# Attention, MLP and top-1 experts on one core: first expert's rows gathered ahead of the last token tile

## The chip, the cores and the metric

The kernel runs on one core of a Trainium2 chip. A core has a matrix engine (TensorE, PE in the profile), two engines for elementwise work that read and write both the on-chip memory (SBUF) and the matrix accumulators (PSUM) (VectorE, DVE; ScalarE, ACT), a third one that works on SBUF and issues indexed transfers (GpSimd, POOL), and an engine that issues the other transfers (SyncE, SP). All run their own instruction queues in order and wait for each other on semaphores. The metric is the device time of one execution in microseconds (us). The kernel before took 568.39 us in the median of three runs (563.79 to 570.07).

## What is computed

Three layers in a chain, in float32:

```python
def reference(q, k, v, w1, b1, w2, w_in, w_out, w_gate, e1, e2, capacity):     # shortened
    x = log1p(abs(i - j)) / log1p(max(i, 1))                  # 576 x 576 positions
    bias = relu(x[..., None] @ w1 + b1) @ w2                  # 32 hidden units, 8 heads
    p = softmax(q @ k.T / 8 + bias)                           # 2 batches, 8 heads, 576 x 64
    x = rows(p @ v)                                           # 1152 tokens x 512
    h = x @ w_in                                              # 512 -> 2048
    x = (h * tanh(log1p(exp(min(h, 20))))) @ w_out            # 2048 -> 512
    logits = x @ w_gate                                       # 8 experts
    e, g = argmax(logits), softmax(logits)[argmax]
    for each expert: the first 288 of its tokens, in order of token:
        out[token] = g * (relu(x[token] @ e1[expert]) @ e2[expert])   # 512 -> 1024 -> 512
```

A token whose expert already has 288 tokens gets zero.

## The kernel before

Tokens go through in five tiles, `it` 0 to 4. Tiles 0 to 3 hold 128 rows of each of the two batches (numbered t = 0 to 7, t = 2 it + batch); the last tile, it = 4 (t = 8), holds the last 64 rows of both. For each tile there are: the bias (hidden layer of 32 units over the distances, `bias_tile`: a relu with a per-partition bias for each group of hidden units, L299 on DVE or L498 on ACT, then matmuls L509 into PSUM, an eviction `rbe`, a round trip through DRAM `bscr`), attention (scores L567 and L570, minimum L584 on DVE, exponential L585 on ACT, transposes L593, products L657), the MLP (products L766 and L799 or L803, with w_in and w_out held as a high and a low f16 half that are made at the start from the weights' loads), and `emit_y` (transposes, gate logits, the argmax as a one-hot row `o3`, the rank of each token within its expert, the table `tbl` of slots scattered to DRAM, and the rows `yscr` of all tokens written to DRAM).

Up to that point the operations are not issued in the order in which they are written. A planner records each operation with its engine, a cost in nanoseconds, the buffers that it reads and writes and other engines that could do it. A table of numbers, `ORDER`, then says in which order the operations are issued; each number is eight times the operation's index plus the chosen alternative. Buffers come from rings: `R2` (row-sized SBUF buffers, `ra*` and `rw*`), `RB` (eight PSUM banks `pb*`, `ps*`), `RBE` and `RX` (the bias evictions and the MLP's input). A buffer is taken again when its last reader is done.

The expert stage stands behind it, in the order as written. `first_slots` gives the token numbers of the first expert's 288 slots: for each tile a one-hot of slots times token number is added up in `acc0` and `acc1` (L1008; one for each batch), the last tile has its own, and nine small matmuls (L1031) with a selector bring the sum to 96 rows by three columns, `gid0` (L1037). Then:

1. `gather(0)`: three indexed transfers of 96 rows of `yscr` each, issued by POOL (L1210).
2. `experts_list`: 14 small DVE operations give the list `lst` of experts that have tokens, which SP and the other engines load into registers.
3. `xt(0, c)`: four transposes on PE for each gathered block (L1223), and a split into a high and a low part (ACT, DVE; L1053, L1054) into `xT0`.
4. `gemm1(0)` (L1233, 96 products of 288 columns, four runs of 24 in the trace), `gemm2` (L1256), the scatter of the results; the loads, gather and weight splits of the next expert run beside them.

The weights of the first expert, `W1`, are split into high (ACT, L1086) and low (DVE, L1087) 128x1024 pieces by planned operations (`first_loads`).

## Time and profile before

| | |
|---|---|
| median of 3 runs | 568.39 us (563.79 to 570.07) |
| the profiled execution | 565.96 us, its span 564.2 us |
| mean granted TensorE clock | 0.949 of full speed |
| TensorE busy | 498.4 us (88%) |
| VectorE, ScalarE, GpSimd busy | 399.6, 349.6, 130.5 us |
| last product of the MLP's second layer ends | 433.57 us |
| first product of gemm1(0) starts | 454.04 us |

The rows below come from one profiled execution, and all times in them are microseconds from the start of its span. "PEclk" is the TensorE clock that was granted in a stretch, as a share of full speed. A row of the timeline gives the start of a run of like instructions, the time from its start to its end, the engine, the line of the kernel, the operation, out<-in, and how many there were (x4); in brackets stands the idle time of the engine before it, and what ended that.

### The profile page before, as it was taken

The page shows a single profiled execution, that of the slowest core. Times are in us where ns is not written, and L with a number is a line of the kernel's source. Part 1 is how long each engine was busy: PE and PEld are TensorE (multiplying, and loading weights), DVE is VectorE, ACT ScalarE, POOL GpSimd, SP SyncE. Part 2 cuts the span into 40 slices and gives each one's busy share as a digit, 9 for nine tenths or more (in the row PEclk, how much of TensorE's full clock was granted, in tenths as well). Part 3 has the DMA queues.
Part 4 walks back from the last instruction along what each step waited for, and adds up shares of the span by engine and source line. Part 5 has one row for each costly group of instructions (what it writes and reads, how often), then busy time and mean ns, then how long its engine had stood idle before and what let it go on. Part 6 is the DMA issues. An engine that isn't in the chain of part 4 may idle for free.

```text
span 564.2 us, 11689 instructions
## 1 busy us (share of the span) xinstructions
PE 498.4 (88%) x4412; PEld 359.6 (64%) x4412; DVE 399.6 (71%) x975; ACT 349.6 (62%) x705; POOL 130.5 (23%) x151
## 2 busy tenths in 40 slices
PE   4545798999999999999979999999998199999975
PEld 2211365686687564465757774699557189999963
DVE  5989999999865678668645875479766653837362
ACT  6879998878565768886726872356543153636251
POOL 4332124113001313100000325025232401131311
PEclk9778599999999999999989999999999579999998
DMA  8996975700200145224360002050006263373711
GB/s 292 377 339 218 362 249 182 279 10 1 81 22 24 66 133 178 86 82 168 111 146 29 1 3 88 3 205 2 1 21 243 70 227 123 105 271 97 283 34 31
DMA packets 28471, 73.96 MB, mean 131 GB/s; under 512 B 5126, under 2 KB 5254, under 8 KB 26352
## 3 DMA queue, kind: packets, MB, share of 16 engines
q1 hardware_dynamic: 26704, 68.95, 36.0%
q0 software_dynamic: 1696, 4.11, 2.4%
q8 instruction: 39, 0.64, 0.5%
q14 instruction: 32, 0.26, 0.2%
HBM read 55.67 MB, written 17.61 MB: 130 GB/s over the span
## 4 chain that ended last, share of the span: by engine, by line
PE 62%; DMA 10%; DVE 7%; issue 5%; ACT 2%; POOL 2%; SPq 0%; POOLq 0%; DVEq 0%; ACTq 0%
PE pb L799 13%; PE pb L766 12%; DMA xg<-yscr,gid 5%; PE ps L567 5%; PE pb L657 4%; PE ps L766 4%; DMA ra<-bscr 3%; PE py L1256 3%; PE pb L593 3%; PE ph L1233 3%; PE pt L1233 2%; PE pb L509 2%; PE pb L803 2%; PE ps L593 2%; PE ps L570 2%
## 5 line engine op out<-in xcount | busy, mean ns | idle before, releaser
L766 PEld LDWEIGHTS <-WIt 128*128 128x128 f16 x960 | 85.2, 98 | 13.2 <-issue 3.0
L766 PE MATMUL pb<-PX,WIt 128*128 128x256 f16 (+1 forms) x720 | 78.5, 264 | 1.1 <-ACT ra L596 1.1
L799 PE MATMUL pb<-WOt,ra 128*128 128x512 f16 x288 | 67.3, 379 | 0.0
L585 ACT ACTIVATE ra<-ra,rm 128x576 f32<-128x576 f32 x58 | 44.8, 774 | 14.2 <-DVE rm L584 14.2
L567 PE MATMUL ps<-AT,rq 64*128 64x512 f32 (+1 forms) x160 | 43.3, 673 | 8.3 <-DVE rm L584 8.3
L509 PE MATMUL pb<-ra,w2s 128*32 128x512 f32 (+16 forms) x232 | 32.2, 531 | 17.0 <-ACT ra L498 10.7
L498 ACT ACTIVATE ra<-AT,stab 128x576 f32<-128x576 f32 (+17 forms) x72 | 44.8, 661 | 3.1 <-DVE AT L299 2.3
L799 PEld LDWEIGHTS <-ra 128*128 128x128 f16 x288 | 27.7, 98 | 29.7 <-issue 1.5
L584 DVE CUSTOM_DVE_ANT_0 ra<-ps,ra 128x576 f32<-128x576 f32 x51 | 37.1, 752 | 12.7 <-DMA ra<-bscr 5.0
L299 POOL TENSOR_SCALAR rw<-rw 128x1024 uint32<-128x1024 uint32 (+1 forms) x19 | 25.8, 1357 | 66.6 <-DMA rw<-wo 28.8
L1256 PE MATMUL py<-HH,W 128*128 128x288 f32 x288 | 40.5, 298 | 0.0
L1054 DVE TENSOR_TENSOR W<-AT,W 128x1024 fp32r<-128x1024 f32 x28 | 33.7, 1223 | 9.3 <-ACT W L1053 4.9
L1256 PEld LDWEIGHTS py<-HH,W 128*128 128x128 f32 x288 | 38.9, 188 | 0.0
L657 PE MATMUL pb<-ra,AT 128*64 128x128 f32 (+1 forms) x640 | 37.4, 266 | 0.0
L657 PEld LDWEIGHTS pb<-ra,AT 128*64 128x64 f32 x640 | 32.2, 137 | 4.2 <-issue 3.4
L302 DVE SCALAR_TENSOR_TENSOR rw<-rw 128x1024 int32<-128x1024 int32 (+1 forms) x26 | 31.9, 1241 | 1.5 <-POOL rw L299 1.1
L593 PE MATMUL pb<-ident,ra 128*128 128x128 f32 x183 | 29.1, 290 | 1.4 <-ACT ra L585 1.0
L570 PEld LDWEIGHTS ps<-AT,rq 128*128 128x128 f32 (+1 forms) x80 | 10.8, 185 | 29.7 <-issue 29.0
L1053 ACT ACTIVATE W<-AT 128x1024 fp32r<-128x1024 f32 x28 | 29.0, 1055 | 0.0
L299 DVE TENSOR_SCALAR ra<-AT,stab 128x544 f32<-128x544 f32 (+16 forms) x46 | 22.6, 508 | 8.2 <-PE pb L799 5.7
L509 PEld LDWEIGHTS pb<-ra,w2s 128*32 128x32 f32 x232 | 7.3, 116 | 32.8 <-ACT ra L498 15.6
L596 ACT COPY ra<-pb 128x384 f32<-128x384 f32 x50 | 22.8, 478 | 6.9 <-PE pb L593 4.6
(404 smaller groups left out, 1084.7 us busy)
## 6 DMA issues: line engine op xcount, KB each, us to landing
AT<-m SPq DMA_DIRECT2D x32, 512.0 KB
bscr<-rbe SPq DMA_DIRECT2D x36, 295.5 KB
ra<-bscr SPq DMA_DIRECT2D x29, 288.0 KB
rw<-wo SPq DMA_DIRECT2D x8, 1024.0 KB
rw<-wi SPq DMA_DIRECT2D x4, 1024.0 KB
WOt<-wi SPq DMA_DIRECT2D x4, 1024.0 KB
AT<-k SPq DMA_DIRECT2D x4, 576.0 KB
out<-ra SPq DMA_DIRECT2D x9, 256.0 KB
```

The costliest lines, as they stand in the source:

```text
L299: eng.tensor_scalar(out=out, in0=in0, scalar1=s1, scalar2=s2, op0=op0, op1=op1)
L498: on_act = lambda h_=h_, g=g: act.activation(h_.t[:, 0:dn], T[:, 0:dn], AF.Relu, bias=stab[:, g:g + 1])
L509: pe.matmul(ps.t[32 * c:32 * c + 32, 0:d1 - d0], w2s, hs[c].t[:, d0:d1], start=True, stop=True)
L567: pe.matmul(s_.t[r, 1024 * i:1024 * i + 512], q_.t[hs, c], kraw[hs, k0 + 576 * bb:k0 + 576 * bb + 512], start=True, stop=True)
L584: op("DVE", c_dve(S), lambda i=i, own=own, m_=m_, b_=b_: dve.tensor_tensor_reduce(out=own(), in0=blk(s_.t[:, 960 * i:960 * i + S]), in1=bl ...
L585: op("ACT", c_act(S, 2), lambda i=i, m_=m_, col=col: act.activation(t_.t[:, S * i:S * i + S], t_.t[:, S * i:S * i + S], AF.Exp, bias=m_.t[ ...
L593: pe.transpose(pa.t[:, P * j:P * j + P], t_.t[:, 384 * n + P * j:384 * n + P * j + P], ident)
L657: pe.matmul(ov[64 * i:64 * i + 64, ct % 2, w * bb:w * bb + w], v_, t_.t[:, at + c0:at + c0 + w], start=n == 0, stop=n == 4)
L766: pe.matmul(ps.t[:, n * f_:n * f_ + n], WI[:, wv, ct, P * ft:P * ft + P], xt.t[:, xv, ct, 0:n], start=i == 0, stop=i == 11)
L799: pe.matmul(y_.t, gv()[:, g2, c:c + P], WO[:, wv, ft], **kw)
L1054: dve.tensor_tensor(out=dst[:, 1], in0=src, in1=dst[:, 0].bitcast(F32), op=ALU.subtract)
L1256: pe.matmul(ps[:, 0:SL], W2[:, wv, ft, P * dt:P * dt + P], HH[:, hv, ft], start=ft == 0 and i == 0, stop=ft == 7 and i == 2)
```

## The change

1. **Rows gathered ahead.** A new function `first_rows`, called with tile 3, counts the first expert's tokens of tiles t = 0 to 7 alone, and makes `gid0` from `acc0` and `acc1` without tile 8 (token numbers are held plus one, so that a slot that is empty so far gives row 0 of `yscr`). The three gathers are issued from there, into buffers of the ring `R2`. So that they don't read what is not written, the rows of tile 8 in `yscr` are set to zero early by two transfers of 64 rows.
2. **The last tile by a product.** `first_slots` no longer gathers. The gathered rows are multiplied by a diagonal matrix `dg` (96 by 288, one where a slot is filled by tiles 0 to 7), which transposes them and clears the empty slots at once (three products of 96 columns for each quarter of the 512 features, L1080), and to the same PSUM bank the product of tile 8's rows with their one-hot of slots is added (L1084, 288 columns, float32). The split goes straight from that bank to `xT0` (L1086, L1087). All of this is planned work now. `gather(0)`, `xt(0, c)` and their transposes fall away.
3. **Order behind it.** `gemm1(0)` stands ahead of the register loads that the branch on the number of experts needs; the loads of the list on SP stand ahead of it as before.
4. **Relus on GpSimd.** The relu of the bias tiles gets POOL as a third engine, and the high part of `W1` gets DVE as an alternative to ACT.
5. **Plan.** `PX` and `RBE` move to a pool of their own, which is closed ahead of `W1` and gives place to `xT0`; the planner's cost of a bias reload is 460000 instead of 294912; and the whole table `ORDER` is another one, made with waits for PSUM banks that several operations share.

```diff
-    416, 144, 152, 160, 176, 136, 168, 120, 200, 184, 112, 192, 64, 208, 128, 0, 16, 8, 304, 408, 72, 216, 232, 224,
+    136, 144, 168, 160, 152, 176, 184, 304, 120, 64, 312, 432, 240, 8, 0, 16, 72, 248, 112, 128, 208, 216, 224, 232,
...
-            op("DVE", c_dve(dn, 0.52, 1), on_dve, r=["T", "stab"], w=[h_], p=["Tfree"], lk=1, alt=[("ACT", c_act(dn, 1), on_act)])
+            on_pool = lambda h_=h_, g=g: ts(pool, h_.t[:, 0:dn], T[:, 0:dn], stab[:, g:g + 1], ALU.add, 0.0, ALU.max)
+            op("DVE", c_dve(dn, 0.52, 1), on_dve, r=["T", "stab"], w=[h_], p=["Tfree"], lk=1, alt=[("ACT", c_act(dn, 1), on_act), ("POOL", c_pool(dn, 0.83, 1), on_pool)])
...
+    def first_rows():
+        pn, pi_ = pl.buf(RB), pl.buf(RB)
+        def f():
+            for b in range(2):
+                for t in range(b, 8, 2):
+                    pe.matmul(pn.t[:, E * b:E * b + E], one, o3[:, t, 1], start=t == b, stop=t == b + 6)
...
+        def f():
+            for c in range(NCH):
+                for j in range(2):
+                    pe.matmul(pv(c), acc[j][:, CS * c:CS * c + CS], sel3[:, j], start=j == 0, stop=j == 1)
...
+            dve.tensor_tensor(out=smsk[:, 1], in0=pw[:, :, 1], in1=smsk[:, 0], op=ALU.mult)
+            dve.tensor_tensor(out=smsk[:, 1], in0=pw[:, :, 0], in1=smsk[:, 1], op=ALU.add)
+            ts(dve, gid0, smsk[:, 1], -1.0, ALU.add, 0.0, ALU.max)
+        for c in range(NCH):
+            x_ = pl.buf(R2)
+            op("POOL", 1100, lambda c=c, x_=x_: pool.indirect_dma_start(out=x_.t[:CS, 0:DM], out_offset=None, in_=yscr, in_offset=bass.IndirectOffsetOnAxis(ap=gid0[:, c:c + 1], axis=0)), r=["gid0", "yscr"], w=[x_], lk=0, late=2500.0)
+            xg0.append(x_)
...
     def first_slots(m_):
...
+        for ct in range(4):
+            ps = pl.buf(RB)
+            cc = slice(P * ct, P * ct + P)
+            def f(ps=ps, cc=cc):
+                for c in range(NCH):
+                    pe.matmul(ps.t[:, CS * c:CS * c + CS], xg0[c].t[:CS, cc], dg.t[:CS, CS * c:CS * c + CS], start=c == 0, stop=False)
+            op("PE", 170 * NCH, f, r=xg0 + [dg], w=[ps])
+            def f(ps=ps, cc=cc):
+                pe.matmul(ps.t[:, 0:SL], y_.t[:, cc], m_.t[:, 0:SL], start=False, stop=True)
+            op("PE", 490, f, r=[y_, m_], w=[ps])
+            op("ACT", c_act(SL, 0, 50), lambda ps=ps, ct=ct: act.activation(W["x"][:, 0, ct], ps.t[:, 0:SL], AF.Copy), r=[ps, "W1"], w=[("xh", ct)], alt=[("DVE", c_dve(SL), lambda ps=ps, ct=ct: dve.tensor_copy(W["x"][:, 0, ct], ps.t[:, 0:SL]))])
+            op("DVE", c_dve(SL), lambda ps=ps, ct=ct: dve.tensor_tensor(out=W["x"][:, 1, ct], in0=ps.t[:, 0:SL], in1=W["x"][:, 0, ct].bitcast(F32), op=ALU.subtract), r=[ps, ("xh", ct)], w=[("xl", ct)])
...
     table(0)
-    gather(0)
     experts_list()
...
-    for c in range(NCH):
-        xt(0, c, (PT + PO)[c % 4])
-    tokens(0)
     for k in range(1, E):
         ev[k] = nc.values_load(lst[0:1, k:k + 1], engines=[mybir.EngineType.SP], min_val=0, max_val=E - 1)
+    gemm1(0)
+    tokens(0)
     nv = nc.values_load(lst[0:1, E:E + 1], min_val=1, max_val=E)
```

Three places in the order show where the instructions stand. The first is POOL's queue at the start, behind its constants. Before, it holds only the first bit operations on the weights as they arrive (`rw`, `WOt`: w_in and w_out; a wait on DMAHW is one for a load):

```order
L299 TENSOR_SCALAR rw0_107<-rw0_107 128x1024 [waits DMAHW5_49]
L299 TENSOR_SCALAR rw0_107<-rw0_107 128x1024
L299 TENSOR_SCALAR rw1_108<-rw1_108 128x1024 [waits DMAHW6_49]
L299 TENSOR_SCALAR rw1_108<-rw1_108 128x1024
L299 TENSOR_SCALAR WOt_105<-WOt_105 128x1024 [waits DMAHW0_49] x2
```

In the changed kernel the same queue begins with relus of the bias (`ra<-AT,stab`), and another one stands behind two loads' worth of weights:

```order
L301 TENSOR_SCALAR ra3_112<-AT_103,stab_88 128x560
L301 TENSOR_SCALAR ra1_110<-AT_103,stab_88 128x448 [waits DVE_49]
L301 TENSOR_SCALAR ra9_118<-AT_103,stab_88 128x576
L301 TENSOR_SCALAR ra0_109<-AT_103,stab_88 128x352 [waits DVE_49,PE_49]
L301 TENSOR_SCALAR WOt_105<-WOt_105 128x1024 [waits DMAHW2_49]
L301 TENSOR_SCALAR WOt_105<-WOt_105 128x1024
L301 TENSOR_SCALAR WOt_105<-WOt_105 128x1024 [waits DMAHW5_49]
L301 TENSOR_SCALAR WOt_105<-WOt_105 128x1024
L301 TENSOR_SCALAR ra0_109<-AT_103,stab_88 128x432 [waits PE_49]
```

In all, 46 relus of the bias moved to POOL (24 fewer on DVE, 22 fewer on ACT). Ahead of the first attention minimum (L584, now L587), DVE has 9 of them instead of 19; ahead of the first exponential (L585, now L588), ACT has 32 instead of 41.

The second place is DVE's queue at the end of the last tile. Before, `gid0` came out behind one low part of `W1` and the last additions:

```order
L1087 TENSOR_TENSOR W1_4305<-AT_103,W1_4305 128x1024 [waits DMAHW4_49,Activation_49]
L299 TENSOR_SCALAR rm6_130<-rm6_130,e0s_177 128x1
L299 TENSOR_SCALAR rw1_108<-sl16_172,rm6_130,ids_175 128x288 [waits DVE_49]
L1008 TENSOR_TENSOR acc1_174<-acc1_174,rw1_108 128x288 [waits DVE_49]
...
L1036 TENSOR_TENSOR smsk_181<-pb1_140,smsk_181 96x3 [waits DVE_49,PE_49]
L1037 TENSOR_TENSOR gid0_182<-pb1_140,smsk_181 96x3 [waits DVE_49]
```

Now `gid0` comes first, and between it and tile 8's one-hot of slots (`rw2<-sl16,rm11`) stand the high and low parts of `W1`, five pieces in all with the one behind it, and tile 8's rank:

```order
L301 TENSOR_SCALAR gid0_185<-smsk_184 96x3 [waits DVE_49]
...
L1071 TENSOR_TENSOR rw2_108<-ident_82,smsk_184 96x288 [waits DVE_49]
...
L1137 CAST W1_4575<-AT_103 128x1024 [waits DMAHW1_49]
L1138 TENSOR_TENSOR W1_4575<-AT_103,W1_4575 128x1024 [waits DVE_49]
...
L1138 TENSOR_TENSOR W1_4575<-AT_103,W1_4575 128x1024 [waits DMAHW0_49,Activation_49]
L1138 TENSOR_TENSOR W1_4575<-AT_103,W1_4575 128x1024
L301 TENSOR_SCALAR rm11_130<-rm11_130,e0s_180 128x1 [waits DVE_49]
L301 TENSOR_SCALAR rw2_108<-sl16_175,rm11_130 128x288 [waits DVE_49]
L1138 TENSOR_TENSOR W1_4575<-AT_103,W1_4575 128x1024 [waits DMAHW5_49]
L1087 TENSOR_TENSOR xT0_4571<-pb0_142,xT0_4571 128x288 [waits Activation_49]
```

The third place is PE's queue ahead of the first expert's `gemm1`. Before, the transposes of the gathered blocks `xg1` and `xg2` (here the later two) and then gemm1 (`ph0<-xT0,W1`):

```order
L1223 MATMUL pt1_4820<-ident_82,xg1_4822 128x96 [waits DMASW2_49]
L1223 MATMUL pt1_4820<-ident_82,xg1_4822 128x96 x3
L1223 MATMUL po0_4817<-ident_82,xg2_4823 128x96 [waits DMASW3_49]
L1223 MATMUL po0_4817<-ident_82,xg2_4823 128x96 x3
...
L1233 MATMUL ph0_4813<-xT0_4824,W1_4305 128x288 [waits Activation_49]
L1233 MATMUL ph0_4813<-xT0_4824,W1_4305 128x288 [waits DVE_49]
```

Now, for each quarter (bank pb4, pb3, pb0, pb2), products of the three gathered blocks (`rw0`, `ra4`, `rw1`; DMASW is a wait for a gather) with `dg`, and the product of tile 8's rows:

```order
L1080 MATMUL pb4_146<-rw2_108,rw0_106 128x96 [waits DMASW0_49,DVE_49]
L1080 MATMUL pb4_146<-rw2_108,ra4_113 128x96 [waits DMASW1_49]
L1080 MATMUL pb4_146<-rw2_108,rw1_107 128x96 [waits DMASW2_49]
...
L1080 MATMUL pb0_142<-rw2_108,rw1_107 128x96
L1084 MATMUL pb0_142<-rw2_108 128x288 [waits DVE_49,Activation_49]
L1084 MATMUL pb3_145<-rw2_108 128x288
L1084 MATMUL pb4_146<-rw2_108 128x288
...
L1084 MATMUL pb2_144<-rw2_108 128x288
L1281 MATMUL ph0_4847<-xT0_4571,W1_4575 128x288 [waits DVE_49]
```

The 12 transposes became 16 products, and gemm1's first product now waits for the last low part of all four quarters.

## Rows read from the trace of the kernel before

**Rows 1.** Windows by stage: busy us (x instructions), clock, DMA share, GB/s.

```profile
core 0: us, PE busy (x) PEld busy (x) DVE busy (x) ACT busy (x) POOL busy (x), PEclk, DMA share, GB/s
0.00:70.00 70.00, 38.19 (x330) 17.55 (x330) 59.15 (x127) 58.82 (x105) 21.20 (x50) 0.78 0.88 317
70.00:434.00 364.00, 355.00 (x3323) 243.99 (x3315) 271.12 (x703) 239.18 (x514) 81.40 (x74) 1.00 0.29 94
434.00:454.00 20.00, 6.01 (x63) 4.51 (x63) 11.63 (x55) 3.47 (x8) 7.01 (x8) 0.60 0.21 57
```

**Rows 2.** Waits of PE up to 434 us: waited for, us, times, longest.

```profile
PE pb L509 <- ACT ra L498: 10.7, 3, 7.5
PE ps L567 <- DVE rm L584: 8.3, 5, 3.2
```

**Rows 3.** Timeline, from the end of the MLP to the first expert.

```profile
433.60 0.69 ACT L862 ACTIVATE rw<-pb,gl 128x512 f32<-128x512 f32 x1 [5.36 <-PE pb L803]
...
436.77 0.23 DVE L299 TENSOR_SCALAR rr<-pb,rr 128x8 f32<-128x8 f32 x1
...
439.91 1.22 DVE L1087 TENSOR_TENSOR W<-AT,W 128x1024 fp32r<-128x1024 f32 x1
...
445.80 8.17 SPq L1203 DMA_DIRECT2D tb<-tbl  x2
445.90 0.16 DVE L1037 TENSOR_TENSOR gid<-pb,smsk 96x3 uint32<-96x3 f32 x1
...
447.08 0.94 POOL L1210 DMA_INDIRECT xg<-yscr,gid  x1 [2.34 <-DVE fl L1166]
...
449.55 0.91 POOL L1210 DMA_INDIRECT xg<-yscr,gid  x1 [0.30 <-issue]
...
452.56 0.90 PE L1223 MATMUL po<-ident,xg 96*128 96x96 f32 x4 [0.31 <-DMA xg<-yscr,gid]
...
454.17 1.96 SPq L1047 DMA_DIRECT2D AT<-m  x4
...
457.68 0.41 ACT L1234 ACTIVATE HH<-ph 128x288 fp32r<-128x288 f32 x1 [3.69 <-PE ph L1233]
```

**Rows 4.** Timeline of PE, first two groups of gemm1(0).

```profile
454.04 5.63 PE L1233 MATMUL ph<-xT,W 128*128 128x288 f32 x24 [0.58 <-ACT xT L1053]
459.50 3.33 PE L1233 MATMUL pt<-xT,W 128*128 128x288 f32 x24
```

**Rows 5.** Windows around the same place (columns as in Rows 1).

```profile
438.00:454.00 16.00, 3.69 (x22) 2.62 (x21) 9.23 (x41) 2.22 (x5) 6.04 (x7) 0.50 0.26 70
454.00:458.00 4.00, 3.96 (x15) 3.66 (x16) 0.63 (x2) 0.32 (x2) 0.00 (x0) 0.50 0.76 212
458.00:460.00 2.00, 2.00 (x15) 2.00 (x15) 1.39 (x2) 1.33 (x3) 0.00 (x0) 0.88 0.98 389
```

**Rows 6.** Timeline of PE: float32 products of 128 columns; transposes of 96 columns.

```profile
62.53 0.79 PE L570 MATMUL ps<-AT,rq 128*128 128x128 f32 x2
...
84.96 0.49 PE L570 MATMUL ps<-AT,rq 128*128 128x128 f32 x2
...
506.87 0.88 PE L1223 MATMUL pt<-ident,xg 96*128 96x96 f32 x8
```

**Rows 7.** Instructions by line, 0 to 60 us: busy us, mean ns | idle before.

```profile
L299 DVE TENSOR_SCALAR ra<-AT,stab 128x560 f32<-128x560 f32 (+13 forms) x19 | 9.7, 544 | 2.0 <-PE pb L509 2.0
L299 DVE TENSOR_SCALAR WOt<-WOt 128x1024 int32<-128x1024 int32 (+1 forms) x3 | 2.1, 690 | 0.0
L498 ACT ACTIVATE ra<-AT,stab 128x464 f32<-128x464 f32 (+15 forms) x41 | 24.8, 667 | 3.1 <-DVE AT L299 2.3 <-PE pb L509 0.5 <-PE ps L509 0.3
```

**Rows 8.** Timeline of the first 40 us: POOL's weight pieces, a pair of DVE's relus.

```profile
12.41 5.05 POOL L299 TENSOR_SCALAR rw<-rw 128x1024 f32<-128x1024 f32 x4 [6.55 <-DMA rw<-wi]
...
13.90 2.47 DVE L299 TENSOR_SCALAR ra<-AT,stab 128x560 f32<-128x560 f32 x2 [1.95 <-PE pb L509]
...
32.91 3.37 POOL L299 TENSOR_SCALAR WOt<-WOt 128x1024 uint32<-128x1024 uint32 x2 [11.89 <-DMA WOt<-wi]
```

93 lines of the change are left out of this document (52 added, 41 removed), and 202 rows, old and new, of the table ORDER.

## The prediction

> **What bounds the kernel now.** I read the windows by stage first [rows 1]. From 70 to 434 us PE is busy for 355 of 364 us at full clock: nothing but fewer products could win more than 9 us there, and the change removes none. PE's idle time lies in two places: 31.8 us in the first 70, and 14 of the 20 us from 434 to 454. The waits of PE [rows 2] name the engines of the start: 10.7 us for ACT's relus, 8.3 us for DVE's minimum L584. Both engines are nearly full there, DVE 59.15 and ACT 58.82 of 70 us [rows 1], and so are the transfers, with a share of 0.88. POOL is busy for 21.20.
>
> The other place is a chain, read in the timeline [rows 3]. I count from T = 433.57, the end of the last product of the MLP. `gid0` is written from 445.90 to 446.06, which is T + 12.5; the first gather is issued at 447.08 and the third at 449.55. PE waits for the last one until 452.56, so it landed 3.0 us after the start of its issue, at T + 19.0. Transposes and split bring gemm1 to 454.04 [rows 4], T + 20.5. With PE nearly idle since T + 4.4, the clock that was granted is half [rows 5]: 0.50 from 438 to 458, 0.88 from 458 to 460, full behind it. So gemm1's first 24 products take 5.63 us and the next 3.33 [rows 4], and the first run ends at T + 26.1. That is the number to beat.
>
> **The change, tail.** What goes: tile 8's one-hot, its addition and the third selector product ahead of `gid0`, the wait of the gathers for it, and the 12 transposes. What comes, step by step:
>
> *gid0.* The argmax of tile 8 ends at 436.77 + 0.23 = T + 3.4, and in the new order stands ahead of `gid0` as before. Then come some 16 small DVE operations of 0.16 to 0.23 us [rows 3], two of them of 288 columns, of which I take 0.3 each: 3 us, and 0.5 for the six selector products and the way to PE and back. `gid0` is at about T + 6.9, 5.6 us earlier than before, while the order alone suggests more: the rows are ahead of tile 8's slots, but not ahead of its argmax.
>
> *Gathers.* Issue 0.4 us later at T + 7.3 and, at the spacing of (449.55 - 447.08) / 2 = 1.24, T + 8.5 and 9.8; the last lands 3.0 later, at T + 12.8, 6.2 us earlier.
>
> *One-hot of tile 8.* This is what is late next, as DVE's row order shows. Behind `gid0` stand four small operations and `dg` (1.2), three small ones (0.5), the copy of a high part (0.69, the price of a single-source piece of 1024 columns [rows 7]), a low part (1.22 [rows 3]), the rank's six (1.1), two more low parts (2.44) and the one-hot's two (0.55): 7.7 us, T + 14.6. If POOL's gathers hold DVE up, T + 15.5.
>
> *Products.* No row shows a float32 product of 96 or 288 columns into such a bank. From above: two of 128 columns take 0.49 at full clock and up to 0.79 at half [rows 6], so 0.25 and 0.40 for one, 0.18 and 0.30 for 96 columns, 0.55 and 0.89 for 288. All 12 and 4 take 4.4 us at full clock and 7.2 at half. From below: transposes of 96 columns, 0.88 / 8 = 0.11 [rows 6] at full clock and 0.90 / 4 = 0.23 at half [rows 3], 288 columns at three times that: 2.6 and 5.4. They are products and no transposes, so I take the upper row. Seven of the first nine follow the last landing: T + 12.8 + 2.1 = T + 14.9, the one-hot is there by then. Before, the clock rose about 4.4 us after steady work began (454.04 to about 458.5 [rows 4, 5]); the same here gives full clock from T + 17.2. By then 2.3 us of the last 6.2 (4 x 0.89 and 3 x 0.30, 4.5 in all) are done; the other 2.2 shrink to 1.4. Products end at T + 18.6. The copy to the high part and the low part take 0.41 each (ACT's 288 columns [rows 3]), 1.0 with the waits: gemm1 starts at T + 19.6, only 0.9 us earlier, but at full clock: its first 24 take 3.33 and end at T + 22.9 instead of 26.1. Gain 3.2.
>
> *Behind gemm1.* PE's two register loads now stand between gemm1 and gemm2. SP's two transfers and its loads of the list span 8.17 us [rows 3], of which I read at most 0.9 for one such load. PE's sequencer runs ahead of it, the list is written by T + 23: 0.3 us is left. SP's list comes later (T + 23 instead of T + 14.5), so the weights of the second expert, asked for at 454.17 = T + 20.6, start near T + 29. Their use is a whole gemm1 and gemm2 away: nothing, and up to 2 us where they meet the second gathers. Sum of the tail: -2.9. Its ends: the products at the lower price, rising early, give -6; at half clock throughout, with gemm1's first run still at 5.63, the products end at T + 12.8 + 2.1 + 4.5 = T + 19.4, gemm1's first run at T + 26.0: nothing.
>
> **The change, start.** DVE loses 10 relus ahead of the first minimum, 10 x 0.51 (9.7 us for 19 [rows 7]) = 5.1 us; ACT loses 9 x 0.60 (24.8 for 41) = 5.4 ahead of the first exponential, but three evictions and three weight pieces now stand ahead of it that came later before, 0.41 [rows 3] to 1.2 each, some 4. So of the two that bound the start DVE is relieved by 5.1 and ACT by 1 to 2 us there, and by the rest later. POOL has room (48.8 us of 70 idle), and a relu there costs about half of its 1.26 us for a 1024-column piece [rows 8]. At most 5 us is to be won, since DVE's evictions, the transfers (0.88 of the time) and POOL's own delay stand behind it; nothing, if the transfers set the pace. I take half: -2.5. The rest of the new plan (order, waits for banks, the dearer bias reloads) can win no more than 9 us between 70 and 434 and may lose as much; no row decides for a sign, and I set it at 0, with 4 either way.
>
> **What speaks against it.** Two relus on DVE took 2.47 us at 13.90 [rows 8] while POOL's four pieces ran from 12.41 to 17.46; the mean of a relu is 0.51 [rows 7], so each lost about 0.7. The Trainium skill, SBUF, section Who interferes with whom, says why: GpSimd shares a pair of ports with VectorE, held for a whole instruction, and a single-source VectorE operation in a two-port mode that meets it is blocked until it ends. The trace agrees with it in that row. With POOL running 21 relus more at the start, 9 relus and 4 weight pieces left on DVE could each lose 0.7, which is 9 us against the 5.1 won.
>
> **Sum.** -2.9 - 2.5 = -5.4 on the profiled 565.96 gives 560.6. The median of the runs shown is 568.39, 2.4 above that execution, so I say **563.0** for the median. What a measurement here can tell from no change is about 1%, 5.7 us.
>
> **The rivals.**
> *More than that (0.2).* The products run at the lower price and the clock is up early (-6), and the start wins all of 5: 568.4 - 11 = 557. For it: DVE and ACT end both waits of [rows 2]. Against it: the one-hot behind four pieces of W1.
> *No change (0.2).* The tail keeps its half clock (nothing won) and the start is paced by transfers: 567 to 570, say 568. For it: 0.88 in [rows 1]. This is also the case that the gathers are ahead on paper only: by the order, `gid0` waits for the same argmax.
> *Slower (0.2).* POOL's queue. A relu of the second bias tile stands behind four pieces of `WOt` from two loads; before, POOL sat 11.89 us waiting for `WOt`, until 32.91, and then worked 3.37 [rows 8]. If that load comes no earlier, the relu ends near 37, PE's products of that tile and all evictions behind it wait, and ACT and DVE stand idle in a stage that they bound. That costs up to 11.9; it decides from the 8 us that the start and the tail would win at best. At 8 to 14 lost in the start, beside the 2.9 of the tail: 573 to 579, or 570 if half of it is hidden; I put it at 574. The blocked ports above add to this case.
> *The forecast (0.4).* Own range 559 to 567.
>
> **How the numbers follow.** Leaving out about one in ten at each end, from half of the second case (below 555) to half of the slower one (above 573): 555 to 573. Faster by over 1% means under 562.7: the 0.2 of the first rival and a little over half of the forecast, 0.42. Slower by over 1% means over 574.1: somewhat over half of the last rival, 0.12. The rest, 0.46, is within 1%.
>
> **What would show it.** The tail: the third gather landing near T + 12.8, the first product of tile 8 near T + 15, gemm1 near T + 19.6 and its first 24 products in 3.3 us instead of 5.63. The start: the first minimum earlier than before, and DVE's and ACT's busy time of the first 70 us down by 3 to 5 us from 59.15 and 58.82, while POOL's rises by 12 or more. I am wrong on the tail if the one-hot or the low parts come later than T + 16, or if the clock stays at half into gemm1; on the start if PE waits for a relu of POOL, or DVE's relus take a microsecond each; and on the middle if PE's idle time from the first minimum to T differs by more than 4 us from the 9 of before.

## The result, and the profile after

| | before | changed |
|---|---|---|
| median of 17 runs | 567.57 us (560.06 to 570.66) | 571.55 us (567.41 to 575.52) |
| ratio to before, 95% interval | | 1.0113 (1.0075 to 1.0151) |
| span of the profiled execution | 564.2 us | 569.2 us |
| mean granted TensorE clock | 0.949 | 0.956 |
| TensorE busy | 498.4 us | 508.4 us |
| VectorE, ScalarE, GpSimd busy | 399.6, 349.6, 130.5 us | 410.0, 334.3, 223.9 us |
| last product of the MLP's second layer ends (T) | 433.57 us | 436.47 us |
| first product of gemm1(0) starts | 454.04 us | 459.57 us |

The changed kernel is slower by 1.1% (4.0 us by the medians, 6.4 by the ratio), where 563.0 and a gain of 5.4 were forecast. The time lies inside the range given; the change has the other sign. Its stages, in the columns of [rows 1]:

```profile
core 0: us, PE busy (x) PEld busy (x) DVE busy (x) ACT busy (x) POOL busy (x), PEclk, DMA share, GB/s
0.00:70.00 70.00, 39.28 (x321) 16.45 (x321) 54.22 (x106) 54.71 (x96) 57.32 (x60) 0.83 0.83 298
70.00:434.00 364.00, 355.83 (x3283) 243.05 (x3284) 280.30 (x701) 225.76 (x493) 137.47 (x107) 1.00 0.30 97
434.00:454.00 20.00, 9.75 (x114) 8.52 (x112) 13.86 (x56) 4.30 (x8) 7.96 (x7) 0.65 0.18 51
```

In the first 70 us DVE and ACT did lose the 4 to 5 us that the relus were to take off them (59.15 and 58.82 before). POOL did not gain 12 but 36. Now PE's waits up to 437 us (waited for, us, times, longest), to be read beside [rows 2]:

```profile
PE ps L512 <- POOL ra L301: 8.1, 1, 8.1
PE pb L473 <- DMA AT<-vm: 6.8, 2, 4.4
PE pb L463 <- ACT ra L500: 5.8, 1, 5.8
PE pb L512 <- POOL ra L301: 5.8, 4, 2.8
PE ps L570 <- DVE rm L587: 3.9, 2, 2.0
PE pb L512 <- POOL rw L301: 2.5, 2, 1.9
```

PE's waits for relus of POOL are 8.1 + 5.8 + 2.5 = 16.4 us, where before it waited for ACT's relus (10.7) and for DVE's minimum (8.3). Most of the new waits took the place of old ones: up to 90 us all waits of PE add up to 33.9 us here and to 32.9 before. So the waits name the engine, and what it costs has to come from the experiments. POOL's timeline of the start shows what it was doing:

```profile
8.88 19.55 POOL L301 TENSOR_SCALAR ra<-AT,stab 128x528 f32<-128x528 f32 x8 [3.14 <-DVE stab L301]
28.50 6.77 POOL L301 TENSOR_SCALAR WOt<-WOt 128x1024 uint32<-128x1024 uint32 x4
35.25 2.82 POOL L301 TENSOR_SCALAR ra<-AT,stab 128x432 f32<-128x432 f32 x1
43.14 12.55 POOL L301 TENSOR_SCALAR ra<-AT,stab 128x432 f32<-128x432 f32 x4
```

Eight relus take 19.55 us. The relu that stands behind four pieces of `WOt` ends at 38.07 (the forecast's "slower" rival said 37), but POOL is not waiting for the load ahead of it, as in [rows 8]: it is busy from 8.88 on. Four relus more end at 55.69, and that is where PE's longest wait ends, in its own timeline:

```profile
55.74 0.90 PE L512 MATMUL ps<-ra,w2s 128*32 128x416 f32 x1 [8.13 <-POOL ra L301]
```

By line, POOL up to 90 us (busy us, mean ns | idle before):

```profile
L301 POOL TENSOR_SCALAR ra<-AT,stab 128x352 f32<-128x352 f32 (+12 forms) x20 | 48.2, 2420 | 4.5 <-DVE stab L301 3.1 <-PE pb L512 0.9
```

One relu costs POOL 2.42 us. DVE's own relus there cost 0.54 before [rows 7]. The other 26 relus on POOL come later, in two groups:

```profile
L301 POOL TENSOR_SCALAR rw<-AT,stab 128x432 f32<-128x432 f32 (+10 forms) x14 | 26.0, 1865 | 28.0 <-PE pb L512 13.4 <-DVE rm L587 10.8 <-DVE WOt L304 3.4
L301 POOL TENSOR_SCALAR ra<-AT,stab 128x320 f32<-128x320 f32 (+8 forms) x12 | 20.2, 1685 | 14.3 <-PE ps L512 6.6 <-PE pb L660 6.6 <-PE pb L512 0.9
```

Their mean is 1.78 us, at about the same width (428 columns, 422 in the start). So of the 2.42 us some 0.6 belong to the crowded start and the rest to the relu itself.

The tail, in the timeline, to be read beside [rows 3] (T = 436.47 here):

```profile
442.85 0.17 DVE L301 TENSOR_SCALAR gid<-smsk 96x3 uint32<-96x3 f32 x1
...
443.94 1.30 POOL L1057 DMA_INDIRECT rw<-yscr,gid  x1 [6.53 <-issue]
...
444.44 0.68 DVE L1137 CAST W<-AT 128x1024 fp32r<-128x1024 f32 x1
445.16 1.23 DVE L1138 TENSOR_TENSOR W<-AT,W 128x1024 fp32r<-128x1024 f32 x1
445.54 1.65 POOL L1057 DMA_INDIRECT ra<-yscr,gid  x1 [0.30 <-issue]
...
447.22 2.36 DVE L1138 TENSOR_TENSOR W<-AT,W 128x1024 fp32r<-128x1024 f32 x2
...
447.49 1.73 POOL L1057 DMA_INDIRECT rw<-yscr,gid  x1 [0.30 <-issue]
...
449.74 0.37 DVE L301 TENSOR_SCALAR rw<-sl,rm 128x288 f32<-128x288 f16 x1
...
451.25 1.17 PE L1080 MATMUL pb<-rw,rw 96*128 96x96 f32 x4 [1.13 <-DMA rw<-yscr,gid]
...
454.34 3.08 PE L1084 MATMUL pb<-rw 128*128 128x288 f32 x6
...
457.90 0.68 PE L1084 MATMUL pb<-rw 128*128 128x288 f32 x2
...
459.06 0.46 DVE L1087 TENSOR_TENSOR xT<-pb,xT 128x288 fp32r<-128x288 f32 x1 [0.70 <-ACT xT L1086]
...
459.57 3.46 PE L1281 MATMUL ph<-xT,W 128*128 128x288 f32 x24 [0.99 <-DVE xT L1087]
```

`gid0` comes when it was expected, T + 6.4. The gathers' issues take 1.30 to 1.73 us instead of 0.91 to 0.94, the last block lands at T + 14.7 (PE goes on at 451.25), the products end at T + 22.1, and gemm1 starts at T + 23.1 instead of T + 20.5 before. Its first 24 products are short, 3.46 us, and end at T + 26.6; before, 5.63 us and T + 26.1. So the tail won nothing.

One warning for all that follows: single profiles of kernels with the same order up to T place T between 432 and 437 us. Times are therefore compared by medians and intervals, and inside a profile by marks that repeat well: the start of attention's first minimum (58.5 to 60.4 us in before and in the seven kernels that keep before's start), and the tail counted from T.

### The profile page after: what moved, and what is told of

Read it like the earlier page. It is cut to its first block, busy times and chain, and to the rows that moved or that the text cites. A ratio compares the mean times of both kernels' runs of the same rounds, so it can differ in the third digit from the quotient of the medians.

```text
span 569.2 us, 11778 instructions
## 1 busy us (share of the span) xinstructions
PE 508.4 (89%) x4433; PEld 364.2 (64%) x4433; DVE 410.0 (72%) x972; ACT 334.3 (59%) x677; POOL 223.9 (39%) x191
## 4 chain that ended last, share of the span: by engine, by line
PE 61%; POOL 13%; issue 12%; DMA 9%; DVE 3%; ACT 1%; SPq 0%; POOLq 0%; DVEq 0%; ACTq 0%
PE pb L802 15%; PE pb L769 12%; POOL ra L301 7%; PE pb L660 7%; DMA xg<-yscr,gid 5%; PE ps L570 5%; PE ps L769 5%; PE pb L596 4%; PE pb L512 3%; PE ps L596 2%; PE ps L573 2%; POOL rw L301 2%; PE pb L806 2%; POOL WOt L301 2%; POOL out L1290 1%
## 5 line engine op out<-in xcount | busy, mean ns | idle before, releaser
L301 POOL TENSOR_SCALAR ra<-AT,stab 128x352 f32<-128x352 f32 (+15 forms) x32 | 68.4, 2144 | 18.8 <-PE ps L512 6.6
L769 PE MATMUL pb<-PX,WIt 128*128 128x256 f16 (+1 forms) x672 | 71.8, 263 | 0.6 <-ACT ra L599 0.6
L588 ACT ACTIVATE ra<-ra,rm 128x576 f32<-128x576 f32 x62 | 47.8, 773 | 30.2 <-DVE rm L587 30.1
L802 PE MATMUL pb<-WOt,ra 128*128 128x512 f16 x276 | 64.5, 379 | 0.0
L587 DVE CUSTOM_DVE_ANT_0 ra<-ps,ra 128x576 f32<-128x576 f32 x53 | 38.4, 751 | 9.1 <-PE ps L573 5.9
L500 ACT ACTIVATE ra<-AT,stab 128x496 f32<-128x496 f32 (+17 forms) x57 | 35.4, 651 | 8.4 <-DVE stab L301 2.7
L301 POOL TENSOR_SCALAR rw<-AT,stab 128x432 f32<-128x432 f32 (+10 forms) x14 | 26.0, 1865 | 28.0 <-PE pb L512 13.4
L660 PEld LDWEIGHTS pb<-ra,AT 128*64 128x64 f32 x660 | 34.0, 137 | 2.7 <-issue 1.7
L1290 POOL DMA_INDIRECT out<-OC,tid x9 | 10.9, 1209 | 61.4 <-DVE OC L1296 33.7
L301 POOL TENSOR_SCALAR rw<-rw 128x1024 uint32<-128x1024 uint32 (+1 forms) x13 | 18.9, 1455 | 36.1 <-DMA rw<-wo 21.0
L769 PE MATMUL ps<-PX,WIt 128*128 128x256 f16 (+1 forms) x288 | 30.4, 259 | 0.0
L573 PEld LDWEIGHTS ps<-AT,rq 128*128 128x128 f32 (+1 forms) x80 | 10.7, 183 | 29.0 <-issue 29.0
```

What stands on the lines that cost most here:

```text
L301: eng.tensor_scalar(out=out, in0=in0, scalar1=s1, scalar2=s2, op0=op0, op1=op1)
L500: on_act = lambda h_=h_, g=g: act.activation(h_.t[:, 0:dn], T[:, 0:dn], AF.Relu, bias=stab[:, g:g + 1])
L587: op("DVE", c_dve(S), lambda i=i, own=own, m_=m_, b_=b_: dve.tensor_tensor_reduce(out=own(), in0=blk(s_.t[:, 960 * i:960 * i + S]), in1=bl ...
L588: op("ACT", c_act(S, 2), lambda i=i, m_=m_, col=col: act.activation(t_.t[:, S * i:S * i + S], t_.t[:, S * i:S * i + S], AF.Exp, bias=m_.t[ ...
L660: pe.matmul(ov[64 * i:64 * i + 64, ct % 2, w * bb:w * bb + w], v_, t_.t[:, at + c0:at + c0 + w], start=n == 0, stop=n == 4)
L769: pe.matmul(ps.t[:, n * f_:n * f_ + n], WI[:, wv, ct, P * ft:P * ft + P], xt.t[:, xv, ct, 0:n], start=i == 0, stop=i == 11)
```

## The experiments

### Which part costs: one part given back, one part alone

**The relus given back.** The changed kernel with each of POOL's 46 relus on the engine that had it before (18 to DVE, 28 to ACT); nothing else. In the table `ORDER` what is left of a number when it is divided by eight is the engine:

```diff
-    714, 898, 858, 842, 546,      # alternative 2: POOL
+    713, 897, 856, 841, 544,      # 0: DVE, 1: ACT
```

> The changed kernel, with the 46 relus that it runs on POOL given back to the engine that ran each before (18 to DVE, 28 to ACT), at the same places of the order; all else as in the changed kernel. Theory 1 (the relus on POOL are the loss: 20 of them took 48.2 us in the first 90 us, and PE waited 13.9 us for them): the last product of the MLP ends at 434 us or earlier instead of 436.5, and the time is 566 to 569. Rival (the new order itself costs it, wherever the relus run): the product ends at 436 to 438 and the time stays at 571 or above, since DVE and ACT get 46 relus back, some 27 us of work between them.

568.37 us, ratio 1.0020 (0.9990 to 1.0049). The loss is gone: the relus on POOL cost 1.0113 - 1.0020 = 0.9%, some 5 us. T lies at 435.4 in its profile, not at the 434 that was expected; one profile does not place T that closely. What is left, order, pool, waits for banks and new tail together, is worth nothing that can be measured.

**The tail alone.** The changed kernel's code with the order of before up to tile 8's argmax (so no relu on POOL), and the changed order behind it.

```diff
-    136, 144, 168, 160, 152, 176, 184, 304, 120, 64, 312, 432, 240, 8, 0, 16, 72, 248, 112, 128, 208, 216, 224, 232,
+    # the order of before, its numbers turned into those of the changed kernel, up to the argmax of tile 8
```

> The order of the kernel before up to the last tile's argmax (with the relus on DVE and ACT where they were), and behind it the tail of the changed kernel: gathers ahead, products, the same order of the last 59 operations. Theory 2 (the new tail wins nothing: products at half clock behind gathers that are issued slowly, and the second expert's weights come late): the last product of the MLP ends within 1 us of 433.6, gemm1 starts some 23 us behind it, and the time is 568 to 571, 0 to 3 above the kernel before. Rival (the forecast of the tail holds, and what was lost lies elsewhere): gemm1 starts 20 us behind it, the time is 564 to 565.

568.80 us, ratio 1.0007 (0.9979 to 1.0035). The tail's -2.9 is not there. T came at 437.2 in the profile, an execution of 571.86 us, and not within 1 us of 433.6. Gemm1 starts at T + 22.3, its first 24 products end at T + 25.7 (before T + 26.1).

**The relus alone.** The kernel before, and the same 46 relus on POOL, in before's places.

```diff
-alt=[("ACT", c_act(dn, 1), on_act)]
+alt=[("ACT", c_act(dn, 1), on_act), ("POOL", c_pool(dn, 0.83, 1), on_pool)]
```

> The kernel before, with its own order and tail, in which the same 46 relus run on POOL. Theory 1: PE waits for POOL's relus for 8 us or more, and the time is 571 to 577. Rival (POOL's relus are harmless, the order is the loss): within 1.5 us of the kernel before, 566 to 569.

592.23 us, ratio 1.0405 (1.0357 to 1.0452): 24 us slower, far above the 571 to 577 expected. PE's waits in that kernel (its relus are L281 and L480), and its first minimum:

```profile
PE pb L492 <- POOL ra L281: 13.1, 3, 6.3
PE ps L550 <- DVE rm L567: 8.5, 5, 3.1
```

```profile
69.21 0.75 DVE L567 CUSTOM_DVE_ANT_0 ra<-ps,ra 128x576 f32<-128x576 f32 x1
```

The first minimum stood at 59.04 before. In an order that was not made for them the same relus lose 24 us; in the changed kernel's own order they lose 5.

### What a relu on POOL costs, and why

**Only the first 20 given back**, those up to 90 us (6 to DVE, 14 to ACT); the later 26 stay on POOL.

```diff
-    714, 898, 858, 842, 546,      # the first 20 alone
+    713, 897, 856, 841, 544,
```

> The changed kernel, with only the first 20 of POOL's 46 relus (those that the trace shows up to 90 us) given back, 6 to DVE and 14 to ACT. If the loss of the relus lies in the start (PE waited 13.9 us for them there): 568 to 569, as with all 46 given back. If it lies in the later tiles (26 relus, PE waited 2.5 us): 571 or more.

569.48 us, ratio 1.0027 (0.9993 to 1.0062). That is close to giving all of them back: most of the loss lies in the start, and the later relus cost little. The first minimum says the same: 63.38 in the changed kernel, 60.75 and 60.53 with all and with 20 given back.

**Four forms of the relu.** The bias as a column or as a constant, one operation or two, by group of hidden units; the sums of the hidden layer are changed by this.

```diff
-ts(pool, h_.t[:, 0:dn], T[:, 0:dn], stab[:, g:g + 1], ALU.add, 0.0, ALU.max)
+g % 4 == 0: tensor_scalar(..., scalar1=0.25, scalar2=0.0, op0=add, op1=max)                 # L503
+g % 4 == 1: tensor_scalar(..., scalar1=stab[:, g:g + 1], scalar2=None, op0=max)             # L505
+g % 4 == 2: tensor_scalar(..., scalar1=0.25, scalar2=None, op0=max)                         # L507
+g % 4 == 3: as before                                                                       # L509
```

> The changed kernel with POOL's relus in four forms on lines of their own, to read what the price of 2.4 us hangs on (bias or the relu itself is left out in three of them): an added number and a maximum; a maximum with the per-partition column alone; a maximum with a number alone; and the full form, column and maximum. If the second operation is what is dear, the two single ones take about half, near 1.3 ns a column as the weight pieces do; if the per-partition column is, the two forms with a number do; if neither, but the meeting with DVE, all four stay near 5 ns a column.

A single execution, 565.48 us, so its time is not compared. By line and shape (busy us, mean ns | idle before), 576 columns of three forms and 432 of the fourth:

```profile
L503 POOL TENSOR_SCALAR ra<-AT 128x576 f32<-128x576 f32 x1 | 2.3, 2292 | 0.0
...
L509 POOL TENSOR_SCALAR rw<-AT,stab 128x576 f32<-128x576 f32 x1 | 2.2, 2215 | 0.0
...
L507 POOL TENSOR_SCALAR rw<-AT 128x576 f32<-128x576 f32 x1 | 1.8, 1822 | 11.3 <-DVE rm L594 11.3
...
L505 POOL TENSOR_SCALAR rw<-AT,stab 128x432 f32<-128x432 f32 x1 | 1.4, 1447 | 0.3 <-DVE ra L786 0.3
```

These rows are single instructions. Over all of a form behind 90 us, the full relu takes 4.0 ns a column, an added constant and a maximum 3.9, a maximum with a constant alone 3.1. So a bias column or a constant makes no difference, and the second operation costs 0.4 to 0.5 us at 576 columns. The form with the column and a maximum alone scatters too much to be placed (1447 ns here, 2698 for the same shape in the start).

What stays is most of it: 1822 / 576 = 3.2 ns a column for one maximum. POOL's pieces of the weights, from which the price was taken [rows 8], are called bit operations in the section on the change, but the kernel has arithmetic there: two multiplications by constants in float32 (`WOt` in rows marked f32, 1339 ns for 1024 columns in the changed kernel, 1.3 a column), or a multiplication and an addition on whole numbers (uint32, 1814 ns, 1.8 a column). So the same instruction, in float32 and with two operations as well, is three times as dear when it adds and takes a maximum. An addition alone in float32 was not run, so how the price divides between the two is known only from the second operation's 0.4 to 0.5 us.

**All 46 relus in the cheapest form**, a maximum with a constant, in the same places of the same queues; the hidden unit's bias is left out.

```diff
-ts(pool, h_.t[:, 0:dn], T[:, 0:dn], stab[:, g:g + 1], ALU.add, 0.0, ALU.max)
+pool.tensor_scalar(out=h_.t[:, 0:dn], in0=T[:, 0:dn], scalar1=0.25, scalar2=None, op0=ALU.max, op1=ALU.bypass)
```

> The changed kernel with GpSimd's 46 relus in the one form that was cheapest in relu_price, a maximum with one constant and nothing added (the bias of the hidden unit is left out there), in the same places of the same queues. If the price of a GpSimd relu is what costs the time, its 20 relus up to 90 us fall from 48.2 us to about 34 to 37 (1.7 to 1.85 each), the first minimum of attention comes near 60 us instead of 63.4, and the time falls from 571.5 to 567 to 569 (a ratio to before of 0.999 to 1.003), as when the relus are given back. Rival: the place of the relus in GpSimd's queue, behind the weights' loads, sets it whatever they cost; then the first minimum stays at 62.5 or later and the ratio at 1.009 to 1.011.

564.42 us, ratio 0.9940 (0.9906 to 0.9974). POOL up to 90 us, and the first minimum:

```profile
L502 POOL TENSOR_SCALAR ra<-AT 128x352 f32<-128x352 f32 (+12 forms) x20 | 32.4, 1640 | 2.7 <-DVE AT L301 1.6 <-DVE rm L587 0.5 <-PE pb L512 0.3
```

```profile
60.51 0.75 DVE L587 CUSTOM_DVE_ANT_0 ra<-ps,ra 128x576 f32<-128x576 f32 x1
```

With the same queue and the same places, a relu of 1.64 us instead of 2.42 makes 7 us of difference by the medians (1.7% by the ratios). PE's waits for relus of POOL up to 90 us fall from 13.9 us to 0.6, and POOL now waits for loads of `WOt` and `rw` (up to 7.6 us at once) and still is not late. So the price counts, and the place behind the loads does not. How much of the difference is the price's is less sure: the first relu need not wait for the column of biases and starts at 7.33 instead of 8.88 us, more than half of the 2.9 us by which the first minimum moves, and the hidden values are others.

The kernel is also 0.8% faster than with the relus given back (0.9940 against 1.0020), some 4.5 us, more than was expected. This is not the gain that the forecast looked for in the start: the first minimum comes at 60.5 here and at 60.7 there. In the two profiles the difference lies between that minimum and T (369.4 against 374.7 us), where PE's idle time explains 2.4 us of it. What earns it stays open.

### Where the tail's gain went

**The splits of W1 ahead of T.** The tail alone, and the high and low parts of `W1` at before's places, ahead of T, so that DVE does little while the gathers are issued.

```diff
-    ... 14376, 14616, 14584, 14552, 14512, ...      # 14456 to 14512: the pieces of W1, among tile 8's work
+    ... 13616, 14472, 13896, ...  13656, 14480, 12136, ...      # where before has them
```

> The kernel with the old order and the new tail (568.8), in which the splits of W1 stand on ACT and DVE where the kernel before has them, ahead of the end of the MLP, instead of behind gid0. Theory 3 (DVE's W1 pieces slow down POOL's issue of the gathers, 1.3 to 1.7 us each instead of 0.93, and so make the rows late): each gather is issued in 0.91 to 0.95, the last one lands within 12.8 us of the MLP's end, gemm1 starts 1 to 2 us nearer to it than the 22.3 of that kernel, and the time is 567 to 568. Rival (the issue is slow for another reason): the same issue times and the same 22.3.

567.67 us, ratio 1.0008 (0.9967 to 1.0048). The gathers:

```profile
440.14 0.94 POOL L1038 DMA_INDIRECT rw<-yscr,gid  x1 [2.21 <-DVE n L302]
441.39 0.93 POOL L1038 DMA_INDIRECT rw<-yscr,gid  x1 [0.31 <-issue]
442.62 0.91 POOL L1038 DMA_INDIRECT ra<-yscr,gid  x1 [0.30 <-issue]
```

All three issues take 0.91 to 0.94. In the tail alone they took 0.94, 1.39 and 0.94, the second of them beside DVE's cast and a low part, and the scatter of the table behind them 1.76 beside two low parts, 1.02 here; in the changed kernel, with the same tail, all three ran beside DVE's pieces and took 1.30, 1.65 and 1.73. ACT's pieces were done before the gathers in both. So it is DVE's pieces that stretch the issue. The Trainium skill, SBUF, section Who interferes with whom, says that an indexed transfer which stalls beside a VectorE operation is one for which GpSimd could not get the shared ports while it writes descriptors; these rows agree with it. The same section infers that a two-input VectorE operation does not do this; the issue of 1.73 us ran beside two of those, so here the measurement decides. But little came of it: the last block lands at T + 13.6, not within 12.8, where it was T + 14.0 in the tail alone and T + 14.7 in the changed kernel, and gemm1 starts at T + 21.6, 0.6 earlier than in the tail alone and not 1 to 2. That is too little to be measured: 14 of the 16 products still stand behind the landing and set the end.

**Another order of the products.** In the changed kernel each quarter waits for all three blocks. Here tile 8's four products stand first (they need no gathered row), then for each block the four products of the four quarters; the one-hot of tile 8 is ahead of `dg`. Nothing else differs from the kernel above.

```diff
-for ct in range(4):
-    for c in range(NCH): matmul(ps, xg0[c], dg)       # 3 products of 96 columns
-    matmul(ps, y_, m_)                                # tile 8, 288 columns
+for ct in range(4): matmul(pss[ct], y_, m_)           # tile 8 first
+for c in range(NCH):
+    for ct in range(4): matmul(pss[ct], xg0[c], dg)   # as each block lands
```

> The same as the run with W1 early, with the products in another order: tile 8's four first, as soon as its one-hot is there, while the gathers are still on their way, then for each gathered block its four products at once; the one-hot stands ahead of the diagonal matrix on DVE. Theory 4 (the tail is bound by the 16 products that run at half clock behind the last landing, 7 to 8 us): only four products are left behind the last landing, gemm1 starts 16.5 to 18 us behind the MLP's end instead of 20.5 (before) and 23 (changed), at full clock: 562 to 564.5. Rival (the time is in what stands behind the products, or the start takes it back): above 566.

564.73 us, ratio 0.9936 (0.9897 to 0.9974). PE's timeline (T = 434.46):

```profile
443.99 4.18 PE L1058 MATMUL pb<-rw 128*128 128x288 f32 x8 [2.61 <-DVE nb L1048]
447.97 2.50 PE L1062 MATMUL pb<-rw,rw 96*128 96x96 f32 x16
450.30 1.06 PE L1062 MATMUL pb<-rw,ra 96*128 96x96 f32 x8
452.77 4.89 PE L1262 MATMUL ph<-xT,W 128*128 128x288 f32 x24 [1.42 <-DVE A L282]
```

Gemm1 starts at T + 18.3. PE works while the gathers fly, and the work behind the last landing (T + 13.7) shrinks from 14 products to the 12 small ones. Four had been expected there and a start at T + 16.5 to 18; tile 8's products, at half clock, last until 447.97 = T + 13.5. Nor does gemm1 run at full clock: the clock had risen (0.89 from 451 to 453), PE then waited 1.42 us, and from 453 to 455 it is 0.50 again, so the first 24 products take 4.89 us. Still, this run is faster than both kernels.

**The expert list while the gathers fly.** The same, with `experts_list` planned ahead of the products instead of behind the split.

```diff
+    op("DVE", 2200, experts_list, r=["cnt", "m64", "k64"], w=["lst"])
-    experts_list()
```

> The same as the run with the products in another order, and the list of experts is worked out while the gathers are on their way instead of behind the last low part. Theory 5 (SP gets the list late in the changed kernel, so that the second expert's weights and rows are late by about 1.4 us): the second expert's gemm1 starts 27.3 to 27.8 us behind the first gemm1 plus gemm2's start, as before, PE waits for no weights there, and the time is 0.5 to 1.5 below that run. Rival (the second expert's stall has another cause): no difference.

563.27 us, ratio 0.9939 (0.9905 to 0.9973): the same as without it. The list, and SP's loads behind it, are not what bounds here.

**gid0 ahead of tile 8's logits.** The additions, `gid0` and the gathers do not need tile 8, so they are moved ahead of its gate logits; the gathered blocks' products stand ahead of tile 8's, and two low parts of `W1` behind the one-hot.

```diff
+    first_rows and the three gathers, ahead of the logits of tile 8 (operations 1545 to 1551)
```

> The order of tail_list, with what belongs to tiles 0 to 7 moved ahead of the last tile's logits: gid0 and the three gathers are issued before the argmax of tile 8, the products of the gathered blocks (block by block) stand ahead of those of tile 8's rows, and two low parts of W1 stand behind the one-hot of tile 8. All work is done. If the start of gemm1 is set by the gathers (issue behind tile 8's argmax, T + 7), they are now issued near T + 4, land near T + 9, the products end near T + 13 and gemm1 starts near T + 14.5 instead of T + 18.3 of tail_order: 560 to 562 us. Rival: tile 8's own chain (argmax, rank, one-hot, and the low parts of W1 now behind it) sets it; then gemm1 starts no earlier than T + 17.5 and the time stays at 563 to 566.

565.15 us, ratio 0.9942 (0.9907 to 0.9978): no faster, although gemm1 starts at T + 15.4 and gemm2 at T + 28.3 (before T + 35.5). PE shows where it went:

```profile
433.81 1.50 PE L787 MATMUL pb<-ra,WOt 128*128 128x128 f16 x24
435.15 0.34 PE L1011 MATMUL pb<-o,one 128*128 128x8 f16 x8
437.36 0.43 PE L1027 MATMUL pb<-sel,acc 128*96 128x2 f16 x6 [1.86 <-DVE acc L999]
437.65 1.56 PE L787 MATMUL pb<-ra,WOt 128*128 128x128 f16 x24
```

The selector products of `gid0` (L1027) stood in PE's queue ahead of the last 24 products of the MLP, and waited 1.86 us for the additions. The MLP's products stop at 435.31 and go on at 437.65, so T itself came 2.3 us later.

**Products that nobody reads, to hold the clock.** The kernel above with 22 products of 288 columns in PE's gaps between T and gemm1.

```diff
+    for i in range(8):
+        pe.matmul(fb.t[:, 0:SL], one, sl16, start=True, stop=True)     # three places: 8, 6 and 8
```

> The kernel ahead, with 22 more products of 288 columns whose result nobody reads, in three of PE's gaps between the end of the MLP and gemm1. If PE's idleness there is why the granted clock falls, and the fall is what makes the products and the first group of gemm1 long, the clock stays at or near full, the float32 products take less, and the first group of gemm1 takes 3.3 us instead of 4.9: 1.5 to 4 us less than ahead. Rival: the clock falls all the same, or the added products stand in the way of the real ones: not less than ahead, up to 2 us more.

564.67 us, ratio 0.9965 (0.9929 to 1.0002): no gain. The windows (clock: third value from the end) show why:

```profile
438.00:442.00 4.00, 3.04 (x34) 2.31 (x31) 1.10 (x8) 0.69 (x1) 2.07 (x3) 0.53 0.21 57
442.00:446.00 4.00, 3.77 (x25) 2.72 (x26) 1.94 (x11) 0.77 (x3) 2.28 (x3) 0.50 0.35 98
446.00:450.00 4.00, 4.00 (x33) 3.44 (x31) 3.05 (x19) 0.00 (x0) 0.45 (x1) 0.50 0.85 157
450.00:454.00 4.00, 4.00 (x19) 3.86 (x18) 3.86 (x16) 0.00 (x0) 0.98 (x1) 0.50 0.48 106
```

The clock had fallen by 440, before T and right behind the wait of 1.87 us for the additions; the first added product ran at 443.56, behind tile 8's logits. The first 14 of the 22 came at half clock too (8 in 2.13 us), and only the last 8, ahead of gemm1, at full (1.14 us). They filled PE and moved the real ones back (gemm1 at T + 17.1). Whether an earlier filler would hold it was not tried.

**The selector products behind the MLP.** The kernel with `gid0` ahead, and only those six products moved behind the last 24.

```diff
-    ..., 1547 (selector products), 1780 (the MLP's last 24 products), ...
+    ..., 1780, 1547, ...
```

> The kernel ahead, with the six selector products of gid0 moved behind the last 24 products of the MLP in PE's queue. In ahead they stood in front of these 24, and PE waited 1.86 us there for the additions into acc (VectorE's one-hots, GpSimd's sums), so that T itself came later by about that; gemm1 followed T by 15.4 us instead of 18.3, and the time was that of tail_order. If that wait is what gave the gain back, gid0 now comes about T + 1.2, the gathers are issued from T + 1.5, the products of the gathered blocks still start with dg near T + 6, gemm1 follows T by 15 to 16 us, and the time falls by the 1.9: a ratio to before near 0.990 to 0.991 (561 to 562 us by a before of 567). Rival: the three microseconds of ahead's tail are lost elsewhere (by the loads of the second expert, or by POOL and DVE in the last tile); then the ratio stays at 0.994.

562.91 us, ratio 0.9881 (0.9842 to 0.9920). The same place (T = 430.63):

```profile
429.13 1.50 PE L787 MATMUL pb<-ra,WOt 128*128 128x128 f16 x24
431.14 0.43 PE L1027 MATMUL pb<-sel,acc 128*96 128x2 f16 x6 [0.51 <-DVE acc L999]
...
436.66 3.73 PE L1061 MATMUL pb<-rw,rw 96*128 96x96 f32 x16 [1.22 <-DVE rw L1052]
440.18 1.91 PE L1061 MATMUL pb<-rw,ra 96*128 96x96 f32 x8
441.89 3.43 PE L1064 MATMUL pb<-rw 128*128 128x288 f32 x8
```

The MLP runs through, gemm1 still starts at T + 15.7, and the kernel is the fastest of all, 1.2% under before: the idea of the change, with no relu on POOL and with the products and `gid0` in other places. The profile is of one of its fastest executions (555.96 us), so T itself is not compared here.

The tails and the times agree when they are put side by side. From gemm2's start on, PE waits for only some 4 to 5 us in each, so what gemm2 wins against T is about what the kernel should win:

| kernel | gemm2 starts | against before | measured (ratio x 568 us) |
|---|---|---|---|
| before | T + 35.5 | | |
| tail alone | T + 35.2 | -0.4 | +0.4 |
| W1 ahead of T | T + 34.5 | -1.0 | +0.5 |
| other order of products | T + 32.6 | -2.9 | -3.6 |
| and the list early | T + 32.9 | -2.6 | -3.5 |
| gid0 ahead | T + 28.3 | -7.3, T later by 2.3 | -3.3 |
| and selectors behind the MLP | T + 28.6 | -7.0 | -6.8 |

The intervals are about 2 us either way, and from gemm2's start to the end the profiles differ by up to 2.8 us (94.9 to 97.7, 95.2 before). Within that each row agrees with its time.

## Why the prediction was wrong

**The start (-2.5) is the term that failed, in its sign, and by the price of one instruction.** The step reads: "a relu there costs about half of its 1.26 us for a 1024-column piece". It cost 2.42 us in the start, nearly four times the 0.63 assumed: 1.78 for the relu as it runs later, and 0.6 more among the other engines' work there. The row behind the price, POOL's weight pieces [rows 8], is two multiplications in float32; the relu is an addition and a maximum. (The same rows also had two pieces at 3.37 / 2 = 1.69 us.) POOL's busy time of the first 70 us rose by 36 of the 48.8 us that it had been idle, and PE waited for it, which the prediction had named as a sign of being wrong: "POOL has room" was true of the assumed price and not of the real one. With the relus given back the loss is gone; with cheaper ones in the same places it is gone too, though there not the price alone differs. The table of engines in the Trainium skill, GPSIMD Engine Reference, section Engine selection, puts an operation with one input on GpSimd at roughly line rate; here the relu took 1.78 us on POOL from 90 us on, and 0.47 on DVE in the kernel before, and the measurement decides. The reading of who waits was right in part: DVE and ACT were relieved by 4 to 5 us, but no run shows that this brings the first minimum forward. It came at 59.0 before, and at 59.8 to 60.8 with the new order and the relus given back or made cheaper.

**"POOL's queue" was the mechanism, and it had 0.2.** The rival put it at 574 in the place where it happened: PE waited for a relu of POOL, and attention's first minimum came at 63.4 instead of 59.0. Its reason was another: it let POOL wait for the load of `WOt`; in the trace POOL never waits there, it is late by its own relus. The assumed 0.63 us kept this case small. Had the price been left open from one piece's 1.26 upwards, 20 relus would have taken 25 us and more of the 48.8, with loads to meet in between, and the case could have been given more weight.

**The ports held by POOL: less than feared.** DVE's nine relus left in the start took 0.66 us each against 0.54; 0.1 lost, where the paragraph on what speaks against the change allowed 0.7.

**The tail (-2.9) came out at nothing, in three steps.**
- *gid0 at T + 6.9* was right (T + 6.4), and so was the first gather at T + 7.3 (7.5).
- *The spacing of 1.24 and the landing at T + 12.8* were wrong by 1.9. The forecast thought of POOL's gathers holding DVE up; DVE's pieces of `W1` held up the gathers. That is 1.1 of the 1.9, for without the pieces the landing is at T + 13.6; the other 0.8 stays open. The one-hot, put at T + 14.6, was done at T + 13.6 and not late.
- *Products to end at T + 18.6* was wrong by 3.5, of which 1.9 is the landing. [Rows 6] were misread: "two of 128 columns take 0.49" is one product, for a float32 product stands in the trace as two instructions. The 12 and 4 products are 24 and 8 rows. At half clock one of 96 columns took 0.46 us (3.73 us for 16 instructions) instead of 0.30, one of 288 columns 1.03 (3.08 for 6) instead of 0.89: 9.6 us for all of them, where 7.2 was said. As was said, 14 of the 16 stood behind the last landing. (The "last 6.2" in that step is 4.5, as its own bracket adds up; the 2.2 left over is right.)
- *Half clock in gemm1* was read rightly: its first run took 3.46 instead of 5.63 us. But the clock was at half for the products that paid for it, 0.50 until 457 = T + 20.5, where T + 17.2 was said. The row for "half clock throughout", gemm1's first run ending at T + 26.0 and nothing won, is close to what the trace shows, T + 26.6.
- *Behind gemm1* no wait was added, as said: gemm2 follows gemm1 without a gap, and from there on PE waits for 4.2 us, 4.4 before.

**The middle and the order, set at 0,** were right: with the relus given back order and tail together are at 1.0020, the tail alone is at 1.0007, and PE is idle for 8.2 us between 70 and 434 where it was 9.0.

In sum, by the ratios: relus on POOL about +5, the tail about 0, the order about 0, against -2.5, -2.9 and 0. The +5 is shown by giving the relus back; the profiles do not show where all of it is lost. PE's waits up to 90 us are only 1.6 us longer than with the relus given back (33.9 and 32.3).

## What to carry to other kernels

Price an instruction that moves to another engine by a row of that operation on that engine, down to its arithmetic: the same opcode in the same type took three times as long with an addition and a maximum as with two multiplications. Where there is no such row, let the price range upwards as well, and ask at which price the idle time of the queue is gone. Count the instructions behind one operation in the program before dividing a row by its count. When work is moved ahead, look at what its own waits hold up in the in-order queues it enters, and let what lands last have the least work behind it: the same idea, in other places, turned 1.1% lost into 1.2% won.
